# A new order for the first 300 steps of a hand-ordered kernel, and another place in PSUM for the state update's products

## The chip, the cores and the metric

The kernel runs on one core of one Trainium2 chip. The time is the device time of one execution in microseconds (us); the median of several runs is compared. A profile, taken in one execution, tells for each engine when every instruction ran: TensorE (PE; its weight loads are PEld), VectorE (DVE), ScalarE (ACT), GpSimd (POOL), and SyncE (SP), whose queue issues all the transfers here.

## The reference

Two blocks follow each other. The first is a gated linear attention with a state per batch and head (4 batches, 8 heads, 768 positions, 48 wide); the second is an MLP over the 3072 tokens (384 to 2048 to 384) with a hard-swish.

```python
for t in range(S):
    state = alpha[:, :, t, :, None] * state + einsum('bhd,bhe->bhde', k[:, :, t], v[:, :, t])
    y[:, :, t] = einsum('bhd,bhde->bhe', q[:, :, t], state)
x = y.transpose(0, 2, 1, 3).reshape(B * S, H * D)
h = x @ w_in
g = h * clip(h + 3.0, 0.0, 6.0) / 6.0
out = g @ w_out
```

The weights arrive as 64-bit floats, and the kernel turns them into 32-bit floats itself, by integer operations on their bits.

## The kernel before, in words

**Chunks.** The recurrence goes in 24 chunks of 128 positions (6 for each batch), numbered j, with all 8 heads in a chunk. A scan over alpha (line 309, `r.j`) gives the products of decays from the end of the chunk, a second scan (line 320, `p.j`) those from its start. k is multiplied by the one (`k.j`), q by the other (`q.j`, both line 332). The scores of the two halves of a chunk (`sc.j`, line 346) are masked (`m.j`, line 356), and `ya.j` and `yb.j` (line 455) multiply values and state by scores and queries. The state goes on by `u.j` (line 429: products of k by token and v, for both halves), `sm.j.b` (lines 437 and 439: the sum with the old state), `st.j` (line 409, on GpSimd: the decay) and `sv.j.b` (line 419: the state put beside the values).

**The first six chunks** differ from the others. Their alpha, k and q are loaded in natural order (`la`, `lk`, `lq`, line 251, 1024 packets of 192 bytes) and turned by TensorE (`ta`, `tk`, `tq`, line 282); `ca.j` copies the turned alpha out of PSUM on ScalarE (line 300), `kb.j` turns k back (line 374) and `ck.j` copies it (line 378). `lv.j` loads the values, `qa.j.b` places queries (line 366).

**Weights.** 16 slices (`w.i`) are loaded into five raw buffers used in turn, so that a later slice waits until an earlier one is done. `d2.i` (magnitude, line 196), `d1.i` (low word, line 186) and, for slices 0, 1, 2 and 4, `dx.i` (sign, line 191) run on ScalarE; `d3.i` on VectorE (lines 203 and 205 for these four, lines 207, 208 and 210 for the others); `d4.i` on GpSimd (line 217) adds the low bits and finishes the slice.

**MLP.** For the first chunk pairs the hidden layer is computed by `fa`, `fb`, `f.g.i` (lines 489 and 478), with `fr` on ScalarE (line 494) and `fg` on VectorE (line 498); `b.c.part` (line 516) is the second product. Later pairs use sums of blocks with fewer products (`M`, `P` and others, lines 600 and 703). `z.m.n` issues n products of an identity matrix whose result nobody reads (line 532).

**What sets the order.** The whole kernel is one list of 1788 words, each of which is a step. Steps are emitted in the order of the list, and each engine, and SP's queue of transfers, takes its own instructions strictly in that order; waits between engines follow from the data. So the list is the schedule, and nothing else decides on it.

**PSUM.** Four banks (`banks`, 512 columns each) serve the recurrence: turned chunks (all columns), scores (columns 0 to 255), the state update's products (columns 0 to 191) and y. A number at the end of a word names the bank (`sc.1.0.2` puts the scores of chunk 1 into banks 0 and 2). Four others serve the MLP. Whoever writes columns waits for the reader of what was there. In `update`, two halves of a chunk go to two banks.

Of the kernel before, what the change touches and what calls it, by code (L numbers as in the profile page):

```python
# [17 lines left out]
def kernel(  # L18
# [33 lines left out]
    B, H, S, D = q.shape  # L52
# [4 lines left out]
    NP = H // 2  # L57
# [3 lines left out]
    G = 2  # L61
    GT = G * C
    HB = C // 2
# [157 lines left out]
    R_t, P_t, Q_t, K_t, kb_t, A_t, xT_t, ps_t = ({} for _ in range(8))  # L221
# [200 lines left out]
    def update(j, *at):  # L422
        for b, i in enumerate(at):
            ps_t["u", j, b] = banks[i][:, 0 : NP * D].rearrange("r (p n) -> r p n", p=NP)
        for p in range(NP):
            for a in range(2):
                for b in range(len(at)):
                    half = slice(HB * b, HB * b + HB)
                    nc.tensor.matmul(ps_t["u", j, b][64 * a : 64 * a + D, p],  # L429
                                     kb_t[j][half, p, 64 * a : 64 * a + D],  # L430
                                     v_t[j][half, b, 2 * p + a, 0:D],
                                     start=True, stop=True)
# [316 lines left out]
    def run(words):  # L749
        for word in words.split():  # L750
            name, *at = word.split(".")
            steps[name](*(int(x) for x in at))

    with tc.manual_schedule():
        run("""z.0.5 z.0.3 z.0.1 z.0.8 qa.0.0 w.0 d2.0 d3.0 la.0 ta.0.0 ca.0 r.0 lk.0 tk.0.1 k.0
               z.0.2 p.0 la.1 ta.1.2 lq.0 tq.0.3 ca.1 r.1 lk.1 lv.0.0 sv.0.0 d1.0 kb.0.0 ck.0 z.0.2
               u.0.2.1 sm.0.0 sv.0.1 q.0 qa.0.1 tk.1.0 k.1 p.1 z.0.2 sc.0.2.3 m.0 la.2 ta.2.0 ca.2
               dx.0 w.2 d2.2 kb.1.0 ck.1 lq.1 r.2 sm.0.1 st.1 tq.1.2 q.1 d3.2 z.0.3 d1.2 dx.2
               lv.1.1 u.1.3.1 sv.1.0 sm.1.0 p.2 sm.1.1 sc.1.0.2 m.1 ya.0.3 yb.0 cy.0 lq.2 w.1 d1.1
               tq.2.1 q.2 d4.2 lk.2 tk.2.3 k.2 fa.2.0 d4.0 st.2 sc.2.0.2 d2.1 d3.1 m.2 dx.1 d4.1  # L760
               qa.1.1 lk.3 la.3 ta.3.1 ca.3 la.4 fa.0.1 sv.1.1 w.3 r.3 ta.4.3 ca.4 r.4 tk.3.1 k.3
               kb.2.0 qa.1.0 d2.3 ya.1.2 yb.1 cy.1 fa.1.2 lq.3 ck.2 d1.3 p.3 d3.3 lv.2.2 u.2.3.2
               sm.2.0 d4.3 fb.2 tq.3.1 q.3 fb.1 qa.2.0 sm.2.1 sv.2.0 st.3 fr.0.2.0 fg.0.2 lk.4
               tk.4.0 sv.2.1 w.5 d2.5 k.4 d3.5 d1.5 qa.3.0 d4.5 qa.2.1 sc.3.1.3 m.3 w.6 d2.6 d1.6
               d3.6 d4.6 lv.3.0 lq.4 w.7 kb.3.2 fb.0 f.0.3.3 kb.4.0 ya.2.1 ck.3 u.3.3.2 sm.3.0
               fr.0.3.1 fg.0.3 fr.0.1.0 fg.0.1 qa.3.1 sv.3.0 sm.3.1 p.4 d2.7 sv.3.1 d1.7 d3.7 d4.7
               f.0.5.0 fr.0.5.1 fr.0.0.0 fg.0.5 fg.0.0 tq.4.3 ck.4 la.5 ta.5.2 f.0.6.3 ca.5 w.4
               d2.4 ya.3.0 yb.3 cy.3 fr.0.6.1 yb.2 cy.2 w.9 d2.9 q.4 qa.4.1 d1.4 d1.9 dx.4 la.6 w.8
               d3.4 r.5 lk.5 w.10 d3.9 p.5 ca.6 fg.0.6 d4.9 w.12 lq.5 lv.4.1 d2.8 d3.8 f.0.7.2 d1.8
               st.4 d4.8 d4.4 w.11 fr.0.7.0 fg.0.7 f.1.7.0 fr.1.7.1 fg.1.7 sc.4.0.2 m.4 f.1.1.1  # L770
               fr.1.1.0 fg.1.1 f.1.3.3 fr.1.3.1 d2.10 d1.10 tk.5.3 f.1.0.2 d2.12 d3.10 d4.10 w.13
               fg.1.3 fr.1.0.0 fg.1.0 k.5 d3.12 lq.6 f.1.6.0 f.1.2.1 u.4.1.0 sm.4.0 d1.12 d4.12
               sv.4.0 qa.4.0 ya.4.2 fr.1.6.1 fg.1.6 w.15 tq.5.3 fa.4.3 sv.4.1 d2.11 kb.5.1 d2.13
               fr.1.2.0 f.1.4.2 fr.1.4.1 d1.11 sm.4.1 q.5 r.6 d3.11 d3.13 fg.1.4 d4.11 lv.5.0 lk.6
               tq.6 p.6 d2.15 d3.15 fg.1.2 d1.13 d4.13 sc.5.0.3 yb.4 f.1.5.0 fr.1.5.1 fg.1.5 tk.6
               m.5 b.1.0.2 fb.4 b.1.1 d1.15 d4.15 st.5 y.5 w.14 la.7 lk.7 cy.4 d2.14 qa.5.1 ck.5
# [3 lines left out]
               lv.6.2 ck.6 u.6.3.0 s.1.3.2 x.2 P.1.2 b.0.3 K.1.1 y.7 s.1.4 s.1.5 y.11 y.3 r.7  # L780
               xc.2.1 x.3 y.4 y.8 xc.2.3 k.7 xc.2.0 xc.2.4 y.9 y.12 y.16 y.13 y.15 P.1.3.3 K.1.2
               P.1.4 bo.1 P.1.5 xc.2.5 G.1.1.1 P.1.6 y.14 y.17 y.19 xc.2.6 sm.6.0 G.1.2.2 y.20
               M.2.0.2 lv.12.1 la.8 O.1.1 O.1.0 ca.8 y.18 y.21 y.23 so.1 G.1.3.3 n.2.0.8 bo.0 lq.7
               lv.7.0 O.1.2 m.6 xc.2.2 xc.2.10 xc.2.7 tq.7 r.8 p.7 xc.2.8 sv.6.1 M.2.15.3 M.2.1
               kb.7.3 n.2.1.9 M.2.16 M.2.2 n.2.2.10 M.2.7.0 n.2.7.11 sm.6.1 xc.2.9 q.7 p.8 M.2.3
               M.2.4 n.2.4.12 M.2.8 o.2.0.0 M.2.5 n.2.5.13 qa.7.0 sv.6.0 st.7 lk.8 O.1.3 lq.8 lk.9
               la.9 la.10 tk.8 tq.8 lq.10 lq.9 ya.6.1 yb.6 M.2.9 z.1.3 M.2.18.1 o.2.1.0 e.2.1.1
               M.2.10 cy.6 ck.7 sc.7.0.2 u.7.1.3 n.2.10.14 M.2.11 qa.7.1 ca.9 la.11 y.22 M.2.6.2
               h.2.1 q.8 m.7 e.2.0.0 h.2.0 n.2.11.15 qa.6.0 n.2.18.10 qa.8.1 M.2.12 M.2.19
               n.2.12.12 M.2.13 sm.7.0 sv.7.1 r.9 k.8 o.2.3.0 sv.7.0 ya.7.0 y.24 o.2.5.0 n.2.13.12  # L790
               o.2.2.0 yb.7 cy.7 sc.8.1.2 xc.3.1 o.2.2.1 e.2.2.1 xc.3.3 o.2.3.1 M.2.14 xc.3.4
               xc.3.0 xc.3.5 o.2.4.0 xc.3.7 xc.3.6 o.2.6.0 P.2.0.1 M.3.0.2 M.2.17 h.2.2 o.2.6.1
               e.2.3.0 h.2.3 o.2.7.0 n.3.0.12 M.3.1 n.3.1.9 e.2.5.1 M.3.7.0 n.3.7.13 xc.3.8 o.2.7.1
               K.2.0.3 xc.3.2 kt.8 e.2.6.0 h.2.6 tk.9 M.3.2 n.3.2.10 e.2.4.0 P.2.1 h.2.4 h.2.5
               s.2.0.14 e.2.7.0 G.2.0.1 h.2.7 M.3.3 M.3.4 n.3.4.8 k.9 s.2.1.11 M.3.8 o.3.0.0 ca.10
               kt.9 P.2.3.3 s.2.2.15 s.2.3.14 lv.8.2 kw.8 kr.8 lk.10 sm.7.1 xc.3.9 M.3.5 n.3.5.11
               K.2.2 e.3.0.1 xc.3.10 M.3.9 o.3.1.0 P.2.2 K.2.1 u.8.0.3 M.3.18.2 s.2.5 M.3.10
               n.3.10.14 n.3.18.15 e.3.1.0 s.2.4 P.2.4 tq.9 h.3.0 st.8 sv.8.0 M.3.11 n.3.11.8 tk.10
               p.9 sm.8.0 q.9 r.10 k.10 qa.9.0 qa.9.1 m.8 sm.8.1 h.3.1 M.3.19 o.3.5.0 kt.10 P.2.5
               G.2.2.0 st.9 M.3.12 sc.9.0.1 qa.8.0 n.3.12.10 o.3.3.0 kw.9 lv.9.0 kr.9 sv.8.1  # L800
               u.9.2.3 sm.9.0 sv.9.1 sv.9.0 G.2.1.2 sm.9.1 st.10 M.3.15.2 M.3.16 M.3.6.3 M.3.13 m.9
               o.3.4.0 o.3.6.0 tq.10 n.3.13.10 o.3.2.0 e.3.4.1 ya.8.2 yb.8 ya.9.3 yb.9 cy.9 M.3.14
               M.3.17 cy.8 xc.4.1 P.2.6 e.3.5.0 G.2.3.3 o.3.2.1 xc.4.3 h.3.4 xc.4.4 o.3.6.1 xc.4.5
               xc.4.0 xc.4.6 e.3.2.1 M.4.0.0 n.4.0.10 P.3.0.1 xc.4.7 o.3.7.0 p.10 h.3.5 o.3.3.1
               xc.4.8 M.4.7.3 M.4.1 xc.4.2 h.3.2 o.3.7.1 K.3.0.2 lk.11 O.2.2 tk.11 e.3.6.0 e.3.3.1
               h.3.3 P.3.1 e.3.7.1 n.4.1.13 M.4.2 ca.11 q.10 h.3.6 r.11 k.11 h.3.7 n.4.7.15 lv.10.2
               lv.11.0 kw.10 sc.10.0.1 kr.10 G.3.0.0 u.10.3.2 sm.10.0 qa.10.1 n.4.2.14 M.4.3 M.4.4
               M.4.8 s.3.0.9 xc.4.9 s.3.2.12 s.3.1.11 P.3.3.2 n.4.4.8 M.4.5 o.4.0.0 e.4.0.0 sv.10.1
               sm.10.1 xc.4.10 kt.11 O.2.0 O.2.3 lq.11 m.10 s.3.3.9 s.3.5 M.4.9 o.4.1.0 P.3.2
               sv.10.0 st.11 n.4.5.11 K.3.2 la.13 M.4.18.0 p.11 tq.11 lk.12 tk.12 K.3.1 M.4.10  # L810
               n.4.10.9 q.11 qa.10.0 n.4.18.12 e.4.1.1 la.12 s.3.4 ca.12 h.4.0 r.12 P.3.5 G.3.2.1
               h.4.1 M.4.11 P.3.4 n.4.11.8 M.4.12 n.4.12.14 qa.11.0 M.4.19 p.12 G.3.1.3 lq.12 kw.11
               O.2.1 tq.12 kr.11 u.11.3 sc.11.0.2 sv.11.0 O.3.1 lk.13 P.3.6 qa.11.1 M.4.6.2 G.3.3.2
               k.12 o.4.3.0 m.11 sm.11.0 sv.11.1 kt.12 M.4.13 n.4.13.14 q.12 o.4.3.1 e.4.3.0
               o.4.2.0 o.4.6.0 h.4.3 o.4.2.1 ya.10.1 ya.11.0 yb.10 yb.11 cy.11 cy.10 xc.5.1 ca.13
               xc.5.3 M.4.15.1 M.4.16 M.4.14 P.4.0.2 o.4.4.0 M.4.17 xc.5.4 o.4.5.0 xc.5.0 xc.5.5
               M.5.0.0 o.4.6.1 K.4.0.3 e.4.2.1 h.4.2 P.4.1 qa.12.1 e.4.4.0 xc.5.6 o.4.7.0 h.4.4
               o.4.7.1 tk.13 n.5.0.14 M.5.1 e.4.7.1 h.4.7 e.4.5.0 xc.5.2 h.4.5 xc.5.7 G.4.0.3
               e.4.6.1 h.4.6 s.4.1.12 s.4.0.11 xc.5.8 r.13 xc.5.9 xc.5.10 k.13 kw.12 kr.12 la.14
               sc.12.2.3 u.12.0.1 sm.12.0 n.5.1.13 M.5.2 n.5.2.15 M.5.7.1 n.5.7.8 P.4.3.3 s.4.2.9  # L820
# [118 lines left out]
```

## Time and profile before

| | us |
|---|---|
| median of 3 runs | 537.83 (537.21 to 538.51) |
| the profiled execution's own time | 537.71 |
| its span, first to last instruction | 535.6 |
| PE busy | 523.6 (98%) |
| DVE busy | 475.1 (89%) |
| ACT busy | 259.7 (48%) |
| POOL busy | 50.4 (9%) |

Between the span and the execution's own time lie 2.1 us in which no instruction of the program runs. Busy shares are means over the span; the stage that the change touches is the first 90 us of it, and there the engines must be read window by window and instruction by instruction. Successive instructions of one engine overlap a little, so the distance from start to start is what counts in a queue. The granted clock of PE is 1.00 throughout in the profile's rows.

### The profile page before, as it was taken

How to read it: one execution, taken by the hardware profiler on the slowest of the kernel's cores; microseconds unless marked ns; L12 is line 12 of the kernel's file. 1: busy time of each engine (PE TensorE's matmuls, PEld its weight loads, DVE VectorE, ACT ScalarE, POOL GpSimd, SP SyncE). 2: the span in 40 equal slices, each digit the busy share in tenths (PEclk: the TensorE clock that was granted, in tenths of full speed). 3: DMA queues.
4: the chain of work that ended last, by engine and by line, in shares of the span. 5: the costliest groups of instructions: out<-in, count | busy, mean ns of one | idle time of the engine just before them, and what ended most of it. 6: DMA issues, size and time to landing. Idle time of an engine off the chain costs nothing.

```text
span 535.6 us, 15166 instructions
## 1 busy us (share of the span) xinstructions
PE 523.6 (98%) x6306; PEld 497.0 (93%) x6306; DVE 475.1 (89%) x839; ACT 259.7 (48%) x513; POOL 50.4 (9%) x71
## 2 busy tenths in 40 slices
PE   7799999999999999999999999999999999999997
PEld 7698886789999999999999999999999999999996
DVE  6999989999999899989999899999999898595381
ACT  3889864302753644543644444642634545553240
POOL 5333435000000000000010000000000000000000
PEclk9999999999999999999999999999999999999999
DMA  9998877006515155254354355055354042100001
GB/s 175 214 250 263 205 218 164 9 1 162 151 28 121 29 120 134 51 139 90 92 118 104 89 122 141 20 126 124 85 137 103 17 97 48 43 3 1 15 16 37
DMA packets 124100, 54.40 MB, mean 102 GB/s; under 512 B 83328, under 2 KB 116864, under 8 KB 124032
## 3 DMA queue, kind: packets, MB, share of 16 engines
q1 hardware_dynamic: 124032, 53.44, 42.4%
q8 instruction: 49, 0.80, 0.7%
q14 instruction: 19, 0.16, 0.1%
HBM read 44.50 MB, written 8.91 MB: 100 GB/s over the span
## 4 chain that ended last, share of the span: by engine, by line
PE 64%; DVE 20%; SPq 5%; DMA 3%; issue 3%; ACT 2%; POOL 2%; DVEq 0%; ACTq 0%; POOLq 0%
PE m_ps L703 28%; PE m_ps L600 24%; PE m_ps L478 4%; SPq L262 3%; PE t_ps L455 3%; DVE R L309 2%; DVE g_sb L498 2%; DVE A L356 2%; DMA v<-in_v_dram 1%; PE t_ps L346 1%; PE m_ps L516 1%; PE t_ps L429 1%; DVE g_sb L537 1%; DVE q L332 1%; DVE t L286 1%
## 5 line engine op out<-in xcount | busy, mean ns | idle before, releaser
L703 PE MATMUL m_ps<-w,g_sb 128*128 128x192 f32 x704 | 122.1, 327 | 0.7 <-ACT m_ps L709 0.6
L606 ACT COPY g_sb<-m_ps 128x512 f32<-128x512 f32 x110 | 63.5, 584 | 113.8 <-PE m_ps L600 97.4
L703 PEld LDWEIGHTS m_ps<-w,g_sb 128*128 128x128 f32 x704 | 113.7, 190 | 1.8 <-ACT m_ps L709 0.9
L703 PE MATMUL m_ps<-rings,g_sb 128*128 128x192 f32 x528 | 91.6, 327 | 0.6 <-ACT u L682 0.6
L703 PEld LDWEIGHTS m_ps<-rings,g_sb 128*128 128x128 f32 x528 | 85.3, 190 | 1.0 <-ACT u L682 0.9
L600 PE MATMUL m_ps<-xc,w 128*128 128x128 f32 x640 | 82.8, 277 | 0.5 <-DVE w L541 0.5
L600 PEld LDWEIGHTS m_ps<-xc,w 128*128 128x128 f32 x640 | 77.5, 192 | 1.7 <-issue 0.6
L494 ACT ACTIVATE r<-g_sb,half 128x512 f32<-128x512 f32 x80 | 56.7, 722 | 29.5 <-DVE g_sb L541 11.7
L498 DVE SCALAR_TENSOR_TENSOR g_sb<-r,g_sb 128x512 f32<-128x512 f32 x80 | 53.6, 683 | 7.2 <-ACT r L494 6.8
L600 PE MATMUL m_ps<-xT,raw 128*128 128x128 f32 x400 | 52.6, 278 | 1.0 <-ACT g_sb L606 0.9
L600 PEld LDWEIGHTS m_ps<-xT,raw 128*128 128x128 f32 x400 | 48.6, 192 | 2.0 <-ACT g_sb L606 1.4
L409 POOL TENSOR_TENSOR st<-sm,R 128x192 f32<-128x192 f32 x20 | 12.9, 644 | 354.4 <-DVE sm L439 305.6
L647 DVE TENSOR_TENSOR g_sb<-g_sb 128x512 f32<-128x512 f32 (+1 forms) x55 | 42.0, 792 | 1.4 <-PE m_ps L703 1.1
L600 PE MATMUL m_ps<-xT,w 128*128 128x128 f32 x320 | 42.0, 276 | 0.0
L600 PEld LDWEIGHTS m_ps<-xT,w 128*128 128x128 f32 x320 | 39.3, 192 | 0.1
L366 ACT COPY A<-q 48x256 f32<-48x256 f32 x88 | 35.6, 404 | 4.9 <-DVE q L332 3.7
L356 DVE TENSOR_TENSOR A<-t_ps,mask 64x256 f32<-64x256 f32 x96 | 36.0, 413 | 0.4
L478 PE MATMUL m_ps<-xT,w 128*128 128x256 f32 x144 | 32.8, 382 | 0.1
L600 PE MATMUL m_ps<-xc,raw 128*128 128x128 f32 x240 | 31.8, 276 | 0.0
L309 DVE TENSOR_TENSOR_SCAN R<-t,ones 128x516 f32<-128x516 f32 x24 | 29.6, 1235 | 1.1 <-ACT t L300 1.0
L478 PEld LDWEIGHTS m_ps<-xT,w 128*128 128x128 f32 x144 | 26.7, 190 | 3.8 <-POOL w L217 0.2
L600 PEld LDWEIGHTS m_ps<-xc,raw 128*128 128x128 f32 x240 | 29.6, 192 | 0.1
(105 smaller groups left out, 724.8 us busy)
## 6 DMA issues: line engine op xcount, KB each, us to landing
raw<-in_moe_w_out_dram SPq DMA_DIRECT2D x8, 768.0 KB, 5.2
raw<-in_moe_w_in_dram SPq DMA_DIRECT2D x6, 768.0 KB, 6.7
v<-in_v_dram SPq DMA_DIRECT2D x48, 96.0 KB, 3.0
out_dram<-oh SPq DMA_DIRECT2D x44, 96.0 KB, 1.7
far<-kq SPq DMA_DIRECT2D x64, 64.0 KB, 2.2
kb<-far SPq DMA_DIRECT2D x64, 64.0 KB, 2.0
aq<-in_alpha_dram SPq DMA_DIRECT2D x36, 96.0 KB, 2.4
qq<-in_q_dram SPq DMA_DIRECT2D x36, 96.0 KB, 2.4
```

The source lines that it names most:

```text
L262: nc.sync.dma_start(out=to[BLK * o : BLK * (o + 1), :, 0 : V * D - skip], in_=t[o // 2, :, :, skip : V * D])
L309: nc.vector.tensor_tensor_scan(out=reverse(R, n - 1, n), data0=reverse(ax, n, n), data1=reverse(ones, n, n), initial=0.0, op0=ALU.mult, op ...
L356: nc.vector.tensor_tensor(out=to[:, a], in0=sc[a][half], in1=mask[half, half].unsqueeze(1).to_broadcast([HB, NP, HB]), op=ALU.mult)
L366: nc.scalar.copy(out=to[:, a], in_=Q_t[j][64 * a : 64 * a + D, :, half])
L455: nc.tensor.matmul(y_of(j, (i + 1) // 2, p)[:, HB * b : HB * b + HB], vb[:, p, e : e + 32], A_t[j][:, b, 2 * p + a], start=(b == 0 and i = ...
L478: nc.tensor.matmul(h[:, f], w1[:, kk, o : o + C], xT_t[g][:, kk], start=(kk == 0), stop=(kk == KT - 1))
L494: nc.scalar.activation(out=to, in_=h, func=AF.Relu, bias=half, scale=1.0 / 6.0)
L498: nc.vector.scalar_tensor_tensor(out=to, in0=r, scalar=1.0, in1=h, op0=ALU.min, op1=ALU.mult)
L600: nc.tensor.matmul(acc[g][i][:, f * C : (f + 1) * C], spots[w][:, f * C : (f + 1) * C], x_of(g, x), start=(first and f == 0), stop=last, s ...
L606: nc.scalar.copy(out=slots[z], in_=acc[g][i])
L647: nc.vector.tensor_tensor(out=out, in0=in0, in1=in1, op=ALU.subtract)
L703: nc.tensor.matmul(to[g], a, rhs[:, f], start=(first and f == 0), stop=(last and f == HF - 1), skip_group_check=True)
```

## The change

The first 300 of the 1788 words are put into another order; the multiset of steps is the same but for the banks named in 30 of them (`ta`, `tk`, `tq`, `kb`, `sc`, `u`, `ya`), and the remaining 1488 words are unchanged. In `update` the products are put into columns 256 to 447 of their banks instead of 0 to 191.

```diff
     def update(j, *at):
         for b, i in enumerate(at):
-            ps_t["u", j, b] = banks[i][:, 0 : NP * D].rearrange("r (p n) -> r p n", p=NP)
+            ps_t["u", j, b] = banks[i][:, NP * HB : NP * (HB + D)].rearrange(
+                "r (p n) -> r p n", p=NP)
...
-        run("""z.0.5 z.0.3 z.0.1 z.0.8 qa.0.0 w.0 d2.0 d3.0 la.0 ta.0.0 ca.0 r.0 lk.0 tk.0.1 k.0
-               z.0.2 p.0 la.1 ta.1.2 lq.0 tq.0.3 ca.1 r.1 lk.1 lv.0.0 sv.0.0 d1.0 kb.0.0 ck.0 z.0.2
-               u.0.2.1 sm.0.0 sv.0.1 q.0 qa.0.1 tk.1.0 k.1 p.1 z.0.2 sc.0.2.3 m.0 la.2 ta.2.0 ca.2
-               dx.0 w.2 d2.2 kb.1.0 ck.1 lq.1 r.2 sm.0.1 st.1 tq.1.2 q.1 d3.2 z.0.3 d1.2 dx.2
-               lv.1.1 u.1.3.1 sv.1.0 sm.1.0 p.2 sm.1.1 sc.1.0.2 m.1 ya.0.3 yb.0 cy.0 lq.2 w.1 d1.1
-               tq.2.1 q.2 d4.2 lk.2 tk.2.3 k.2 fa.2.0 d4.0 st.2 sc.2.0.2 d2.1 d3.1 m.2 dx.1 d4.1
-               qa.1.1 lk.3 la.3 ta.3.1 ca.3 la.4 fa.0.1 sv.1.1 w.3 r.3 ta.4.3 ca.4 r.4 tk.3.1 k.3
...
-               st.4 d4.8 d4.4 w.11 fr.0.7.0 fg.0.7 f.1.7.0 fr.1.7.1 fg.1.7 sc.4.0.2 m.4 f.1.1.1
-               fr.1.1.0 fg.1.1 f.1.3.3 fr.1.3.1 d2.10 d1.10 tk.5.3 f.1.0.2 d2.12 d3.10 d4.10 w.13
-               fg.1.3 fr.1.0.0 fg.1.0 k.5 d3.12 lq.6 f.1.6.0 f.1.2.1 u.4.1.0 sm.4.0 d1.12 d4.12
-               sv.4.0 qa.4.0 ya.4.2 fr.1.6.1 fg.1.6 w.15 tq.5.3 fa.4.3 sv.4.1 d2.11 kb.5.1 d2.13
-               fr.1.2.0 f.1.4.2 fr.1.4.1 d1.11 sm.4.1 q.5 r.6 d3.11 d3.13 fg.1.4 d4.11 lv.5.0 lk.6
-               tq.6 p.6 d2.15 d3.15 fg.1.2 d1.13 d4.13 sc.5.0.3 yb.4 f.1.5.0 fr.1.5.1 fg.1.5 tk.6
-               m.5 b.1.0.2 fb.4 b.1.1 d1.15 d4.15 st.5 y.5 w.14 la.7 lk.7 cy.4 d2.14 qa.5.1 ck.5
+        run("""lk.0 la.0 la.1 z.0.8 z.0.3 w.0 ta.0.2 z.0.5 ca.0 r.0 d2.0 tk.0.1 k.0 lq.0 z.0.2 la.2
+               ta.1.2 kb.0.1 z.0.2 w.2 lk.1 w.1 p.0 z.0.3 d3.0 d1.0 lv.0.0 ca.1 ta.2.3 r.1 ck.0
+               tq.0.2 ca.2 lq.1 q.0 lk.2 tk.1.0 dx.0 sc.0.1.2 d2.2 sv.0.0 r.2 lv.1.1 qa.0.1 p.1 d1.2
+               z.0.2 la.3 k.1 d2.1 d4.0 m.0 d3.2 ya.0.0 u.0.3.1 dx.2 sm.0.0 kb.1.3 d3.1 sm.0.1
+               sv.0.1 tq.1.2 yb.0 q.1 d1.1 cy.0 lq.2 ck.1 p.2 tk.2.1 st.1 sc.1.2.0 w.3 u.1.3.0
+               sm.1.0 dx.1 fa.0.1 ta.3.3 k.2 sv.1.0 d4.2 fa.2.0 qa.1.0 ca.3 m.1 lv.2.2 lk.3 kb.2.2
+               sv.1.1 sm.1.1 w.5 r.3 qa.1.1 d4.1 lq.3 st.2 tq.2.1 q.2 ya.1.0 yb.1 d2.3 p.3 cy.1
...
+               fr.1.3.1 d1.8 k.5 fr.1.1.0 d2.12 fg.1.1 f.1.6.0 f.1.2.1 lk.7 d4.4 ck.4 lv.4.1
+               fr.1.0.0 d3.12 d4.8 lv.5.0 u.4.2.0 sc.4.3.0 sc.5.2.1 d1.12 fg.1.3 ca.6 w.11 d4.12
+               st.4 fa.4.3 fr.1.6.1 fg.1.6 fg.1.0 d2.11 m.4 f.1.4.2 fb.4 f.1.5.0 w.15 sm.4.0 r.6
+               d1.11 d4.10 fr.1.4.1 sv.4.1 d2.15 d3.11 m.5 sv.4.0 fg.1.4 b.1.0.2 fr.1.2.0 d3.15 w.13
+               d4.11 w.14 d2.13 lq.6 lk.6 p.6 b.1.1 fr.1.5.1 d3.13 d1.13 sm.4.1 d1.15 ya.4.3 yb.4
+               d4.15 fg.1.5 tq.6 kb.5.0 fg.1.2 d4.13 tk.6 st.5 y.5 z.0.1 cy.4 d2.14 qa.5.1 ck.5
                b.0.0.1 fr.0.4.0 d3.14 k.6 q.6 ca.7 fg.0.4 d1.14 d4.14 x.0 y.1 y.10 b.0.1 y.0 y.2
...
```

Both lists hold 26 of the identity products of `z`. In the list of before the first words of the DMA queue are w.0, la.0, lk.0, la.1, lq.0, lk.1, lv.0; in the new one they are lk.0, la.0, la.1, w.0, lq.0, la.2, w.2, lk.1, w.1, lv.0.

## The prediction

> **What bounds the kernel now.** First view: the page's busy table, then the table of windows over the first 160 us, because only the first 300 of 1788 steps are reordered (they end near 90 us).
>
> ```profile
> PE 523.6 (98%) x6306; PEld 497.0 (93%) x6306; DVE 475.1 (89%) x839; ACT 259.7 (48%) x513; POOL 50.4 (9%) x71
> 10.00:20.00 10.00, 6.87 (x103) 5.46 (x104) 9.75 (x18) 7.30 (x12) 0.04 (x1) 1.00 1.30 234
> 50.00:60.00 10.00, 9.93 (x164) 8.24 (x163) 9.80 (x15) 9.74 (x15) 4.63 (x5) 1.00 0.79 226
> 100.00:110.00 10.00, 10.00 (x156) 6.44 (x155) 10.00 (x14) 1.67 (x4) 0.00 (x0) 1.00 0.01 2
> ```
>
> In the rows the columns are PE, PEld, DVE, ACT, POOL busy of 10 us, clock, DMA share and GB/s. DVE is at 97% or more from 10 us on; PE has room only in the first two rows. Second view, the waits: what PE and DVE wait for up to 160 us, and PE's two late waits in the timeline.
>
> ```profile
> DVE w L203 <- ACT w L196: 2.4, 1, 2.4
> DVE s L439 <- PE t_ps L429: 1.2, 1, 1.2
> DVE R L309 <- ACT t L300: 1.0, 1, 1.0
> 127.84 0.91 PE L600 MATMUL m_ps<-xc,w 128*128 128x128 f32 x6 [0.47 <-DVE w L541]
> 156.44 1.73 PE L703 MATMUL m_ps<-w,g_sb 128*128 128x192 f32 x9 [0.16 <-ACT m_ps L709]
> ```
>
> DVE, once started, is idle for 0.96 us (before 9.26) and 1.16 us (before 72.38), then not at all until 157, and PE's only waits between 52 and 157 are for DVE's results or for ACT behind them. So DVE's place in its queue at step 300 is carried to 157, and PE, which is nearly without a gap behind that, carries it to the end. PE alone being early gives nothing beyond the 0.47 that it waits at 127.
>
> Third view, POOL beside DVE.
>
> ```profile
> 81.22 1.18 DVE L320 TENSOR_TENSOR_SCAN P<-t 128x516 f32<-128x516 f32 x1
> 82.32 1.75 DVE L207 TENSOR_SCALAR w<-w 128x768 f32<-128x768 f32 x1
> 81.65 2.01 POOL L217 TENSOR_TENSOR w<-raw 128x768 int32<-128x768 int32 x1 [0.19 <-POOL kq L257]
> 28.03 1.86 POOL L217 TENSOR_TENSOR w<-w,raw 128x768 int32<-128x768 int32 x1 [0.75 <-ACT raw L191]
> 29.36 1.62 DVE L309 TENSOR_TENSOR_SCAN R<-t,ones 128x516 f32<-128x516 f32 x1
> 89.98 0.55 DVE L207 TENSOR_SCALAR w<-w 128x768 f32<-128x768 f32 x1
> ```
>
> L217 (d4) came up during a scan, ran when the scan ended, and L207, otherwise 0.55 to 0.61, took 1.75: DVE stood still until POOL was done. The scan at 29.36 lost 0.40 in the same way (1.62 against 1.22). The scores' mask (L356), L332 and L498, which read PSUM, keep their duration beside L217.
>
> **The budget of DVE.** From d3.0 (6.57) to d3.14, step 306 (89.98), are 83.41 us. In them: idle 0.96 + 1.16; lost to POOL 0.40 (r.3), 0.39 (d3.1: first op 1.09 for 0.70), 1.14 (d3.15), and 0.28 (d3.0's first op, 0.98 for 0.70, beside POOL's memsets). Sum 4.33, so the work is 79.1. The new order has the same DVE steps. Its start: the first loads are now k, alpha, alpha, then w.0, so d3.0 can no longer run ahead of r.0 in the time in which DVE has nothing else. PE starts with z.0.8 and z.0.3, 22 passes, at 1.47. The first pass takes 0.375 and the next ones 0.213 each (they drop to 0.112 at 6.96), so ta.0 starts at 1.84 + 21 x 0.213 = 6.3; three of its four passes are slow, the last starts at 6.96. ca.0 came 0.31 after that pass before, and takes 0.59: r.0 at about 7.9 (9.26 before). The alpha load is second of three small ones, 1.2 us apart in the landings of before, and is there near 5. DVE would end at 7.9 + 79.1 = 87.0 if it never waited; before it was 89.98. **The new order may wait 3.0 us before it loses.**
>
> A sentence for the rule that speaks on this start: the Trainium skill, "TensorE: Matmul & The Clock Gate", Part 1, puts the change to full rate around 4 us into sustained matmuls, give or take 0.5; by it (5.5 instead of 6.96) r.0 would start some 0.6 earlier, an estimate from that page. Here the passes change 5.5 us after the first, and the row is taken.
>
> **The waits of the new order**, walked from start-to-start rows (r 1.36 to 1.5, p 1.14, k and q 0.60, halves d3 1.36, m 1.50, sm 0.27):
> - a) d4.0. DVE: r.0 7.9, k.0 9.3, p.0 9.9, d3.0 11.0, r.1 12.4, q.0 13.8, r.2 14.4, p.1 15.8. ACT: ta.2 stands behind kb.0, which needs k.0 (9.9): 10.05 + 0.47 + two fillers of 0.45 and 0.67 = 11.6; ca.2 12.25, dx.0 (1.94) to 14.8. So L217 comes up in r.2's scan, as at 81.65, and p.1 waits. Between 0 (ready after 15.8, then it runs beside k.1 and m.0, which read PSUM) and 1.86 (all of L217). By the d3.15 row, 1.14 of a 1.47 L217: 1.5 of 1.86.
> - b) sm.1.0 after p.2: u.1 now waits for ck.1, behind sv.0.1, d1.1 and cy.0 on ACT: 0.71 + 0.93 + 0.48 + 0.58 after sm.0.0, and 0.63 from u's start to sm. 0 to 0.7; 0.6.
> - c) r.3 against d4.1, which stands behind d4.2 on POOL: 0 to 1.2; 0.4 as before.
> - d) d4.15 stands ahead of d4.13 now and waits for d1.15; it comes up near 84, inside d3.13's three ops (83.4 to 85.6). 0 to 1.4; by the d3.15 row 1.2.
> - e) small ones (m.2, d3.9 for w.9, whose load waits for d4.6 on SP, q.5, m.4): 0.2 with a), 1.0 without, since DVE then arrives earlier.
> The 1.16 wait for u.4 goes: u.4 is ahead of fa.4 and f.1.4 as before, but sm.4.0 is now behind m.4. What is late next there is sc.4, which stands behind u.4 on PE and which m.4 needs; it is in e).
> Sum 3.9: DVE reaches d3.14 at 90.9, **0.9 later**.
>
> The other queues. PE: 26 fillers before and after, at no cost. It is idle 4.7 us up to 31 us before; afterwards fa.0 starts at 24.6 without a), 26.1 with it, and counting the products behind (f 2.7, fa 1.34) PE is 0.7 earlier or 0.3 later at tk.4. SP: the loads land in the order of issue; the set up to la.5 that landed by 44.15 is the same set up to lq.4, so DMA gains nothing as a whole. lv.0 goes from seventh place of the loads to tenth, landing near 18.4 (13.2 before); that is covered, since ya.0 waits for m.0 (19 or later); uncovered it costs up to 5 us. w.14 now stands before lq.6 and lk.6 on SP and waits for d4.11 (near 79); they land by 87, tq.6 and tk.6 need them from 87 on: 0 to 0.5, taken as 0.
>
> Column 256: no instruction more or less. A u may be written beside scores that wait for their mask. In steps 301 to 1788 nothing waited for that bank, as PE's waits there name DVE's w and g_sb, ACT's g_sb, m_ps and u (a kept sum) alone: 0, within 0.1 either way.
>
> **Rivals.**
> 1. POOL's additions miss the scans: dx.0 ends after 15.8 and d4.15 outside d3.13. For it: a shift of ACT against DVE by 1 us is enough for the first, and most L217 before ran beside steps that read PSUM (28.03 under m.2 until the scan came). Against: both are needed. DVE's waits fall to 0.6 to 2.2, but PE's 0.7 plus the 0.47 of slack limit the gain to 1.2: 536.6. Chance 0.20.
> 2. One of a) and d) is absent: without a) the waits are 3.4 (b 0.7, c 0.5, d 1.2, e 1.0), without d) 2.7, so 0.4 later or 0.3 earlier: 537.5 to 538.2. Chance 0.16.
> 3. Slower: p.2 loses to d4.2. st.1 starts 0.51 after sm.0.1 and runs 0.52; d4.2 stands directly behind it, at 1.02. p.2 arrives at 0.27 + 0.60 = 0.87, during st.1. If POOL goes on without a gap, p.2 waits all of d4.2, 1.7; it decides whether p.2 starts before 1.02. Against: at 26.6 a DVE op that waited went ahead of the next L409. 0.9 + 1.7: 540.4. Chance 0.20.
> 4. PE runs at half rate again. Between the filler behind sc.0 (16.0) and ya.0 (19.1, or 20.6 with a) PE has nothing for 3.1 to 4.6 us; before, its longest idle stretch was 0.96, and the rate stayed at 0.112. If slow passes (0.213) come back for the 5.5 us of the start, PE loses up to 2.7, of which three transposes (0.4 each) lie on DVE's path at least: 1.2 to 2.7, taken as 2.0. 0.9 + 2.0: 540.7. Chance 0.14. The Trainium skill, the same page, "HAM oscillation", warns of idle gaps over 3.4 us; no run here shows one yet.
> That the reorder has no effect at all can't be: the first load already differs.
>
> **How the numbers follow.** The forecast, a) to e) as valued, has 0.30. The profiled execution took 537.71 (span 535.6 and 2.1 around it), 0.12 under the median 537.83; 0.9 on the median is 538.7. About 0.2% (1.08 us) is what can be told from no change. The forecast's own range is 537.9 to 539.4 (b, c, e at their ends), so a third of its chance is beyond 538.9: 0.10 slower, 0.20 same. Same: 0.20 + 0.16 = 0.36. Slower: 0.10 + 0.20 + 0.14 = 0.44. Faster: 0.20. The range takes in half of rivals 1 and 4: 536.5 to 540.7.
>
> **What would show it.** The first scan of DVE near 7.9; the second p's start behind a L217 near 17 rather than at 15.8; a d3 with an op of 1.7 to 2.0 near 84; d3.14 near 91; PE's wait at 127 larger. Wrong, if no scan stands beside L217 (rival 1), if a scan after st.1 starts after 26 (rival 3), or if passes near 21 us are 0.213 apart (rival 4).

## The result and the profile after

The changed kernel took 541.27 us, the median of 6 runs (540.04 to 542.88), against 537.75 (537.21 to 538.51) for the kernel before on the same chip: a ratio of 1.0070 with a 95% interval of 1.0058 to 1.0083. The forecast was 538.7, its range ended at 540.7. The profiled execution of after took 540.35, with a span of 538.3.

First the table of windows of after. The columns are PE, PEld, DVE, ACT and POOL busy, the granted clock, the DMA share and GB/s.

```profile
10.00:20.00 10.00, 6.43 (x117) 5.15 (x117) 9.73 (x15) 9.13 (x12) 1.97 (x1) 0.75 1.21 247
20.00:30.00 10.00, 8.98 (x157) 7.94 (x150) 9.01 (x16) 7.11 (x13) 4.74 (x4) 0.73 1.11 231
40.00:50.00 10.00, 9.56 (x105) 7.97 (x105) 9.78 (x18) 8.34 (x16) 2.93 (x2) 1.00 0.49 112
```

The granted clock was 1.00 in these rows before. Now it is 0.75 and 0.73: the records have it at half from 15.1 to 25.3 us. The third row shows the DMA engines half idle between 40 and 50 us, which matters further down. The waits that DVE makes up to 95 us, "what for" behind the arrow, with total, count and longest:

```profile
DVE R L309 <- ACT t L300: 2.9, 2, 2.7
DVE g_sb L499 <- ACT r L495: 0.7, 1, 0.7
DVE w L207 <- ACT w L196: 0.6, 1, 0.6
DVE q L332 <- PE t_ps L282: 0.5, 1, 0.5
DVE s L440 <- PE t_ps L430: 0.2, 1, 0.2
```

The first line is mostly the start (2.70 before the first scan at 6.88). Waits tell only half: what POOL takes shows as long instructions. The timeline of after, DVE and POOL:

```profile
14.30 1.97 POOL L217 TENSOR_TENSOR w<-w,raw 128x768 int32<-128x768 int32 x1 [6.73 <-ACT raw L191]
14.77 2.60 DVE L320 TENSOR_TENSOR_SCAN P<-t 128x516 f32<-128x516 f32 x1
23.31 0.69 DVE L332 TENSOR_TENSOR q<-t_ps,P 128x512 f32<-128x512 f32 x1 [0.48 <-PE t_ps L282]
23.38 1.84 POOL L217 TENSOR_TENSOR w<-w,raw 128x768 int32<-128x768 int32 x1
24.03 2.28 DVE L320 TENSOR_TENSOR_SCAN P<-t 128x516 f32<-128x516 f32 x1
26.48 0.36 DVE L440 TENSOR_TENSOR s<-t_ps,st 128x192 f32<-128x192 f32 x1 [0.17 <-PE t_ps L430]
85.46 1.46 POOL L217 TENSOR_TENSOR w<-raw 128x768 int32<-128x768 int32 x1 [2.51 <-ACT raw L186]
85.51 1.83 DVE L207 TENSOR_SCALAR w<-w 128x768 f32<-128x768 f32 x1
92.84 0.55 DVE L207 TENSOR_SCALAR w<-w 128x768 f32<-128x768 f32 x1
```

Three times a DVE instruction stands still for more than 1 us until an L217 ends: p.1 at 14.77 and p.2 at 24.03 (2.52 and 2.45 to the next start, 1.14 where nothing holds them) and d3.13's first at 85.51 (1.87, 0.59 otherwise). Behind p.2, sm.1.0 (26.48) still waits 0.17 for u.1, whose products do not need p.2: with p.2 short and PE no faster, sm.1.0 would hardly have come earlier. The last row is d3.14, step 306: 92.84, which is 2.86 later than before. Third, PE in the timeline of after:

```profile
14.48 0.66 PE L282 MATMUL t_ps<-ident,rings 128*128 128x128 f32 x4 [2.38 <-DMA rings<-in_k_dram]
16.13 1.22 PE L533 MATMUL m_ps<-ident 128*128 128x128 f32 x4
21.30 1.11 PE L374 MATMUL t_ps<-ident,k 128*128 128x128 f32 x4 [1.01 <-DVE s L438]
22.21 1.06 PE L282 MATMUL t_ps<-ident,rings 128*128 128x128 f32 x4
91.45 3.81 PE L517 MATMUL m_ps<-w,g_sb 128*128 128x384 f32 x11 [1.05 <-DVE g_sb L499]
```

PE waits 2.38 for the load of k of chunk 1, and from 15.1 on four passes take 1.06 to 1.22 in place of 0.60 to 0.66. At 91.45 it waits 1.05 for DVE's fg.1.2; the same product started at 88.20 before. Of these 3.24 us PE makes up some 0.5: the product P.2.0.1 starts at 151.66 (148.91 before) and the last, P.11.6, at 532.67 (529.92), both 2.75 later. The wait of 0.47 at 127 that PE had before is gone.

So the delay that DVE has near d3.14 is carried to the end, and it arises before that step. It is not carried as predicted: the prediction looked for a longer wait of PE at 127, but PE is late from 91.45 on and has no wait in the profile between there and 159. Over all the profiles that follow, the profiled execution's time is 537.3 plus the delay of d3.14 against 89.98, within 0.25 us.

### The profile page after: what moved, and what is told of

Read it like the earlier page. It is cut to its first block, busy times and chain, and to the rows that moved or that the text cites. A ratio compares the mean times of both kernels' runs of the same rounds, so it can differ in the third digit from the quotient of the medians.

```text
span 538.3 us, 15147 instructions
## 1 busy us (share of the span) xinstructions
PE 524.8 (97%) x6306; PEld 497.9 (92%) x6306; DVE 477.0 (89%) x839; ACT 259.5 (48%) x513; POOL 50.3 (9%) x71
## 3 DMA queue, kind: packets, MB, share of 16 engines
q1 hardware_dynamic: 124032, 53.44, 42.2%
## 4 chain that ended last, share of the span: by engine, by line
PE 69%; DVE 14%; DMA 6%; SPq 4%; ACT 3%; issue 3%; POOL 0%; DVEq 0%; ACTq 0%; POOLq 0%
PE m_ps L704 32%; PE m_ps L601 25%; PE t_ps L456 3%; PE m_ps L517 3%; SPq L262 3%; DVE g_sb L499 2%; PE m_ps L490 2%; DMA g_sb<-in_moe_w_in_dram 2%; PE t_ps L346 1%; PE t_ps L430 1%; ACT r L495 1%; DMA raw<-in_moe_w_in_dram 1%; DVE g_sb L538 1%; DVE A L356 1%; DVE R L309 1%
## 5 line engine op out<-in xcount | busy, mean ns | idle before, releaser
L495 ACT ACTIVATE r<-g_sb,half 128x512 f32<-128x512 f32 x80 | 56.7, 722 | 30.1 <-DVE g_sb L542 11.7
L320 DVE TENSOR_TENSOR_SCAN P<-t 128x516 f32<-128x516 f32 x24 | 31.8, 1326 | 0.2
```

The costliest lines, as they stand in the source:

```text
L320: nc.vector.tensor_tensor_scan(out=P_t[j], data0=aX[j % 2][:, 0:n], data1=ini[j % 2], initial=0.0, op0=ALU.mult, op1=ALU.add)
L495: nc.scalar.activation(out=to, in_=h, func=AF.Relu, bias=half, scale=1.0 / 6.0)
```

## The experiments

Every kernel below the first row was timed in five rounds beside the kernel before on the same chip, whose medians were 537.27, 537.34 and 537.49. The third column is against the one that goes with the run. The last three columns are from the one profiled execution: the first scan of DVE (r.0), d3.14, and the mean granted clock.

| kernel | median us | against before | ratio, 95% interval | r.0 at | d3.14 at | clock |
|---|---|---|---|---|---|---|
| after | 541.27 | +3.52 | 1.0070 [1.0058, 1.0083] | 6.88 | 92.84 | 0.990 |
| after_again | 540.77 | +3.43 | 1.0062 [1.0050, 1.0074] | 7.16 | 93.51 | 0.991 |
| col256_only | 537.36 | +0.09 | 1.0001 [0.9992, 1.0009] | 9.38 | 89.89 | 1.000 |
| fill_pe | 539.74 | +2.47 | 1.0045 [1.0029, 1.0061] | 8.03 | 92.69 | 1.000 |
| late_dx0 | 540.18 | +2.91 | 1.0053 [1.0041, 1.0065] | 7.81 | 92.52 | 0.994 |
| d415_last | 541.16 | +3.89 | 1.0067 [1.0053, 1.0082] | 7.35 | 91.88 | 0.990 |
| no_d40_d42 | 538.65 | +1.31 | 1.0014 [1.0001, 1.0027] | 7.33 | 91.63 | 0.994 |
| loads | 539.89 | +2.55 | 1.0044 [1.0029, 1.0059] | 6.85 | 91.49 | 0.990 |
| pause_pool | 540.66 | +3.17 | 1.0053 [1.0038, 1.0067] | 7.77 | 94.75 | 0.991 |
| all_four | 538.36 | +1.02 | 1.0017 [1.0008, 1.0025] | 7.25 | 90.74 | 1.000 |
| five | 536.98 | -0.51 | 0.9987 [0.9978, 0.9996] | 7.75 | 89.15 | 1.000 |
| five_less_fill | 537.69 | +0.20 | 1.0001 [0.9992, 1.0010] | 7.83 | 90.55 | 0.997 |
| before_no_fill | 538.12 | +0.63 | 1.0013 [1.0004, 1.0022] | 8.62 | 90.73 | 0.994 |

In after, after_again and the nine kernels from fill_pe to five_less_fill nothing ahead of r.0 differs, and yet r.0 comes anywhere from 6.85 to 8.03. It goes with the moment at which PE gets its full rate, which the clock records put at 4.79 in loads (r.0 at 6.85), at 4.86 in after (6.88) and at 7.68 in fill_pe (8.03). So d3.14 of two rows can't be compared without r.0, and the single medians differ from that of after by little more than their intervals; gains below about 1 us are estimates.

### The two parts of the change: col256_only

The order of before with the products in columns 256 to 447.

```diff
-            ps_t["u", j, b] = banks[i][:, 0 : NP * D].rearrange("r (p n) -> r p n", p=NP)
+            ps_t["u", j, b] = banks[i][:, NP * HB : NP * (HB + D)].rearrange(
+                "r (p n) -> r p n", p=NP)
```

> The order of before with the column change alone. If the column place costs or gains anything by itself, the time moves by a good part of the 3.5 us between the two kernels (540 or more). If the order alone does it, 537.75 within 0.5. I expect the second.

537.36 against 537.27, within an interval of some 0.5 us. In the old order the column costs nothing that can be told, so the loss is put down to the order; the column was not tested in the new order alone.

### PE's clock: fill_pe

Two groups of identity products are put where PE waits: ten behind tq.0, and ten in place of two behind sc.0.

```diff
-               tq.0.2 ca.2
+               tq.0.2 z.0.10 ca.2
...
-               z.0.2 la.3
+               z.0.10 la.3
```

> The changed kernel with 10 identity products more behind tq.0, where PE waited 2.4 us for k of chunk 1, and 10 instead of 2 behind sc.0, where it waited for the mask. If the half clock of PE between 15.1 and 25.3 us is a main cost, the granted clock reads 1.00 throughout, passes near 21 us are 0.11 apart instead of 0.21, q.1 no longer waits (0.48) and the time falls by 1 to 2 us, to 539 to 540; the spread of the runs shrinks too. If GpSimd's additions beside the scans are all of it, the clock reads 1.00 and the time stays within 0.4 of the changed kernel's 541.3.

The windows of fill_pe, columns as above, and its p.2 in the timeline:

```profile
10.00:20.00 10.00, 9.06 (x132) 8.55 (x131) 9.87 (x15) 9.07 (x11) 2.25 (x1) 1.00 1.22 245
20.00:30.00 10.00, 7.93 (x178) 7.14 (x175) 9.79 (x18) 7.49 (x14) 4.39 (x3) 1.00 1.05 214
```

```profile
24.33 1.87 POOL L217 TENSOR_TENSOR w<-w,raw 128x768 int32<-128x768 int32 x1
24.40 2.88 DVE L320 TENSOR_TENSOR_SCAN P<-t 128x516 f32<-128x516 f32 x1
```

The half rate is gone, so the cause of it was PE's idle time. The clocks of the other executions agree: 0.997 to 1.000 in all six of fill_pe, 0.990 or 0.991 in all six of after. The gain is about 1.0 of 3.5 in the medians; the spread did not shrink as expected (538.04 to 541.52). The profile's d3.14 is only 0.15 earlier, but its r.0 came 1.15 later, so from r.0 on 1.30 are gained. Part is lost again: with PE at full rate p.2 arrives right behind the start of d4.2 and waits for all of it (2.81 to the next start instead of 2.45), and d3.12 waits 0.49 for slice 12.

### The locks one by one: late_dx0, d415_last, no_d40_d42, pause_pool

late_dx0 moves dx.0 behind d2.2 on ACT, so that d4.0 is ready later.

```diff
-               tk.1.0 dx.0 sc.0.1.2 d2.2 sv.0.0
+               tk.1.0 sc.0.1.2 d2.2 dx.0 sv.0.0
```

> The changed kernel with dx.0 behind d2.2 on ACT, so that d4.0 comes up near 16.2, while p.1 runs, and not while r.2 does. If GpSimd's addition held p.1 back, p.1 takes 1.14 instead of 2.52 from start to start, the mask of chunk 0 starts near 16.5 instead of 17.9, and the time falls by about 1.4 us or more (PE's idle stretch ahead of ya.0 is shorter as well); 539.9. If the loss is the clock alone, p.1 is short but the time stays within 0.4 of 541.3.

p.1 is free (1.12 to the next start, at 15.47 with L217 behind it at 15.72), and m.0 comes 0.70 earlier (17.18), although r.0 came 0.93 later. But d3.15 comes only 0.27 earlier (82.04) and the median gains about 0.5 where 1.4 were expected, inside the intervals. The timeline of late_dx0 shows p.1, and where the rest went:

```profile
15.47 1.21 DVE L320 TENSOR_TENSOR_SCAN P<-t 128x516 f32<-128x516 f32 x1
57.94 0.69 DVE L499 SCALAR_TENSOR_TENSOR g_sb<-r,m_ps 128x512 f32<-128x512 f32 x1 [0.53 <-ACT r L495]
69.78 0.56 DVE L207 TENSOR_SCALAR w<-w 128x768 f32<-128x768 f32 x1 [0.43 <-ACT w L196]
```

At fg.0.6 (57.94) DVE is still 0.71 ahead of after. Then d3.12 (69.78; 69.98 in after) waits 0.43 for slice 12, whose load SP issued at 63.66 (62.28 in after): DVE came earlier, the slice did not. That need not come from the edit: in after_again, the unchanged kernel, slice 12 was issued at 64.91 and d3.12 waits 0.71.

d415_last puts d4.15 behind d4.13.

```diff
-               d4.15 fg.1.5 tq.6 kb.5.0 fg.1.2 d4.13 tk.6
+               fg.1.5 tq.6 kb.5.0 fg.1.2 d4.13 d4.15 tk.6
```

> The changed kernel with d4.15 behind d4.13 on GpSimd, so that it does not stand beside d3.13. If d4.15 held VectorE up there, d3.13's first operation takes 0.6 instead of 1.83 and everything behind it is 1.2 us earlier: 540.1. If PE is the bound at that place, the operation is short and the time the same, 541.3.

In the profile d3.13 keeps its 0.6, d3.14 is 0.96 earlier and the execution took 539.03. That was the fastest of its six, and the median, 541.16 where 540.1 was expected, is no better than that of after. The profile shows the lock removed; that this alone gains time is not shown.

no_d40_d42 leaves out d4.0 and d4.2, and with them the low bits of weight slices 0 and 2: a bound for what the locks at p.1 and p.2 cost together.

```diff
-               d2.1 d4.0 m.0
+               d2.1 m.0
...
-               sv.1.0 d4.2 fa.2.0
+               sv.1.0 fa.2.0
```

> The changed kernel without GpSimd's additions d4.0 and d4.2: the low bits of weight slices 0 and 2 are left out, nothing else. If these two additions beside p.1 and p.2 cost what VectorE stood still for them (1.4 and 1.1), p.1 and p.2 take 1.14 each and the time falls by 2.5, to 538.8. If a later wait is a floor that takes early gains back (in the three variants so far VectorE comes to d3.15 at 82.0 to 82.3 whatever it gained before), VectorE is 2 us or more earlier at m.2 (35.8 in the changed kernel), but again at 82 at d3.15, and the time falls by less than 1.

m.1 comes at 25.75 (27.36 in after), the median falls by 2.1, more than any other single edit gives, although the clock is still at half from 16.0 to 22.9. Behind it waits appear that after does not have, or has at less than 0.2: 0.79 for sm.1.0, 0.51 for r.3, 0.49 for q.3, 0.52 for fg.0.5. The single executions range from 535.95 to 539.58, the widest spread of all the kernels.

pause_pool puts seven small memsets of a spare tile on POOL between st.1 and d4.2, so that p.2 can start first.

```diff
+    spare_pool = consts.tile([C, 64], FP, tag="spare_pool", name="spare_pool")
+    def pause(n):
+        for _ in range(n):
+            nc.gpsimd.memset(spare_pool, 0.0)
...
-               st.1 sc.1.2.0
+               st.1 zp.7 sc.1.2.0
```

> The changed kernel with seven small memsets of a tile of their own on GpSimd between st.1 and d4.2 (0.8 us), so that p.2 asks first and d4.2 runs behind it, beside sm.1.0, k.2 and m.1, which read PSUM. If p.2 loses to d4.2 only because d4.2 starts 0.6 us ahead of it, p.2 takes 1.14 instead of 2.28 from start to start, m.1 starts 0.8 to 1.1 earlier, and the time falls by up to 1.1; by less, near 0.3, if the loads for d3.9 and d3.12 hold VectorE back again. If the memsets themselves hold the scan, p.2 takes 2 or more.

The timeline of pause_pool, DVE and PE:

```profile
24.71 1.23 DVE L320 TENSOR_TENSOR_SCAN P<-t 128x516 f32<-128x516 f32 x1
27.69 0.36 DVE L440 TENSOR_TENSOR s<-t_ps,st 128x192 f32<-128x192 f32 x1 [1.75 <-POOL w L217]
26.84 0.69 PE L430 MATMUL t_ps<-v,kb 64*48 64x48 f32 x32
```

The scan takes 1.23 again, and the next step, sm.1.0, waits 1.75. The view names POOL because L217 ended last; but sm.1.0 needs u.1, which PE ended at 27.53, and it does not need the slice: in five, below, it starts 0.08 after an L217 did, and in after, five and five_less_fill as here it starts 0.15 to 0.16 after u.1's last product ended. So the half clock holds DVE at sm.1.0 with p.2 free, as the 0.17 in after already said. The two causes lie over each other there, and neither fill_pe nor pause_pool can win much alone. How long the wait is depends on the execution: here the half rate ran from 16.95 to 27.19, later than in after, and m.1 came later, not earlier as expected. (The profiled execution, 541.98 with d3.14 at 94.75, was the longest of its five.)

### The gate at slice 9: loads

w.9 behind lq.5, and la.6 ahead of d4.9.

```diff
-               sm.3.0 w.9 m.3
+               sm.3.0 m.3
...
-               lq.5 yb.3
+               lq.5 w.9 yb.3
...
-               la.7 d4.9 la.6
+               la.7 la.6 d4.9
```

> The changed kernel with two loads moved in SP's queue: w.9, which waits for d4.6, behind w.4, lk.5 and lq.5, and la.6 ahead of d4.9 in the list, so that w.12 does not stand behind it. If the loads are the floor, the waits of d3.9 (0.56), fg.0.6 (0.69) and d3.12 shrink by 1 us or more in all and VectorE comes to d3.15 before 81.5; the time falls by 0.5 to 1.2. If they are not, d3.15 stays at 82 or later and the time within 0.4 of 541.2.

In after, w.9 waits on SP for d4.6, with every later load behind it: it is issued at 47.19 and landed at 53.44, and the third row of after's windows shows the DMA engines idle meanwhile. In the timeline of loads the same two steps (before the first, 0.56 of waiting in after, before the second 0.69) have no wait:

```profile
53.72 0.56 DVE L207 TENSOR_SCALAR w<-w 128x768 f32<-128x768 f32 x1
57.41 0.69 DVE L499 SCALAR_TENSOR_TENSOR g_sb<-r,m_ps 128x512 f32<-128x512 f32 x1
```

d3.15 comes at 81.15 in place of 82.31, with r.0 and the half rate at the same place as in after (6.85, and 15.03 to 25.27). The median gains about 0.9. This is the cleanest pair of profiles here.

### All together: all_four, five, and one filler less

all_four joins fill_pe, late_dx0, d415_last and loads; five adds the seven memsets; five_less_fill is five with z.0.2 instead of z.0.10 behind sc.0.

> The changed kernel with the four edits together: more identity products, dx.0 behind d2.2, d4.15 behind d4.13, and the two loads moved. If early delays, floor and d4.15 act one after the other, it gains more than the sum of the single ones (1.3, 0.9, 0.2 and that of the loads): d3.15 before 81, d3.14 near 89.5 to 90.5, 537.0 to 538.3, about the kernel before. If something else keeps VectorE back, d3.15 stays at 82 and the time above 539.

all_four is still 1.02 over before, just outside what was expected. p.2 comes 0.08 behind d4.2 now and loses all of it, and sm.2.1 waits 1.74 for u.2, in the midst of which PE stands 1.84 without a wait that the profile shows.

> The kernel with four edits and this pause as a fifth. In the one with four, p.2 came 0.08 us behind d4.2 and stood still for 1.7 us. If the pause flips that, p.2 takes 1.14, and d3.14 comes near 89.0 unless the 1.7 us wait of sm.2.1 on PE stays: 90 with it. 536.5 to 537.5: level with the kernel before or 0.1% below it. If something else bounds, d3.14 stays at 90.7 and the time at 1.0017 of before.

The timeline of five, POOL and DVE:

```profile
22.61 1.40 POOL L737 MEMSET spare_pool<- 128x64 f32 x7
23.97 3.66 POOL L217 TENSOR_TENSOR w<-w,raw 128x768 int32<-128x768 int32 x2
22.71 1.23 DVE L320 TENSOR_TENSOR_SCAN P<-t 128x516 f32<-128x516 f32 x1
24.05 0.36 DVE L440 TENSOR_TENSOR s<-t_ps,st 128x192 f32<-128x192 f32 x1
```

p.2 runs its 1.23 beside the memsets, and d3.14 comes at 89.15, 3.69 before that of after and 0.83 before that of before. The median, 536.98, is 0.13% under the kernel before (interval 0.04% to 0.22%), which is below the 0.2% named as what can be told from no change: level with it, perhaps a little faster. PE's 1.84 within u.2 is absent here, although PE has the same instructions as in all_four, so not all of the difference between these two is the memsets'. Against after the five edits are worth 3.9 to 4.0 (3.43 or 3.52 over before, and 0.51 under it).

> The same five edits with only the identity products behind tq.0 and 2, not 10, behind sc.0. If the 1.84 us in which PE issued nothing inside u.2 came from the place at which those 16 more passes put it in PE's instruction stream, it is gone or elsewhere, and sm.2.1 does not wait. If PE's clock needs both groups, a half-rate stretch is back and the time is 1 us above the kernel with both.

537.69 against 536.98 for five on the same chip: one group of eight identity products more is worth about 0.7 (the two intervals just meet). The window row of five_less_fill shows why:

```profile
20.00:30.00 10.00, 9.36 (x180) 8.48 (x184) 8.00 (x15) 7.74 (x15) 6.02 (x11) 0.83 1.03 238
```

q.1 waits 0.48 and sm.1.0 waits 0.89 for PE again. The granted clock is 1.000 in all eleven executions of five and 0.994 to 0.999 in those of five_less_fill.

### Fillers in the old order: before_no_fill

The kernel before without its four groups behind r.0 (nine products).

> The kernel before without the four groups of identity products behind r.0 (9 products, 2.2 us of PE up to 19 us). If sparse work on PE is what brings the half rate, PE reads 0.5 in a stretch between 12 and 26 us, and the time rises by 0.5 to 2 us. If the rate falls only after PE stands still for most of a 3.4 us stretch, which before's longest idle stretch (0.96, about 1.7 without the products) does not come near, it stays at 1.00 and the time within 0.4 of before.

It loses 0.63. The windows of before_no_fill, and PE's longest wait in its timeline:

```profile
10.00:20.00 10.00, 5.13 (x89) 3.78 (x90) 9.16 (x17) 7.32 (x12) 0.04 (x1) 0.97 1.30 234
20.00:30.00 10.00, 9.87 (x198) 9.32 (x199) 9.39 (x19) 9.16 (x13) 6.34 (x5) 0.69 1.01 215
```

```profile
19.94 1.03 PE L429 MATMUL t_ps<-v,kb 64*48 64x48 f32 x29 [1.62 <-ACT kb L378]
```

The clock is at half from 19.35 to 26.17, and the mean is 0.987 to 0.994 in all eleven executions (0.997 to 1.000 in those of before). So the old order stands on its fillers too. The half rate is not a property of the new order but of any start in which PE is left idle enough.

### The spread: after_again

The kernel after, unchanged.

> The changed kernel once more, for a second profile: its runs lie between 540.0 and 542.9, and the profiled one was at the low end with 2.75 us of delay at the end of PE's chain. If the rest of the spread comes from where the windows of PE's clock fall, the half-rate stretch begins at another time than 15.1 and the delay at d3.14 differs from 2.86 with it; if it comes from somewhere behind 100 us, d3.14 is at 92.8 again and the span differs.

540.77; its ratio of 1.0062 lies in the interval of the first time. Its d3.14 is at 93.51, with the half rate from 15.67 to 25.91 and with 0.94 before fg.0.6 and 0.71 before d3.12: at least part of the differences from run to run arises before step 306.

## Why the prediction was wrong, by its own steps

**What held.** DVE's budget up to d3.14 was the right account; the delay there was carried to the end, though through PE from 91.45 on and not through a wait at 127; column 256 costs nothing in the old order; POOL's L217 does come up in r.2's scan and inside d3.13. The Trainium skill, "SBUF — State Buffer", "SBUF: two separate sides", says that a VectorE instruction in a two-port mode, or one with two inputs from SBUF where the GpSimd instruction reads SBUF, shares one pair of ports with GpSimd as an exclusive lock, and that the second to start fully blocks. The trace agrees: instructions 2.60, 2.28 and 1.83 long for 1.23, 1.23 and 0.55, while the scan beside the memsets, which read nothing, kept its 1.23.

**The sum.** From its first scan DVE took 85.96 to d3.14 (6.88 to 92.84); with 79.1 of work that is 6.86 of waiting, against 3.9 forecast.

| term | forecast us | measured us |
|---|---|---|
| start of r.0 | 7.9 | 6.88 |
| a) d4.0 at p.1 | 1.5 | 1.38 |
| b) sm.1.0 for u.1 | 0.6 | 0.17 |
| c) r.3 | 0.4 | 0.16 |
| d) d4.15 at d3.13 | 1.2 | 1.28 |
| e) small ones | 0.2 | 2.25 (r.4 beside L217 0.35, d3.9 0.56, fg.0.6 0.69; 0.65 is left, in pieces below 0.2) |
| rival 3, d4.2 at p.2 | 0 | 1.14 |
| rival 4, q.1 for PE at half rate | 0 | 0.48 |

Of the 2.96 us by which the waiting was put too low, e) makes up 2.05 and the two rivals 1.62; a), b) and c) were put 0.79 too high. The 1.14 of rival 3 is what p.2 lost, not what its removal would gain, since b) would take its place.

**First failed step: the rivals.** Rivals 3 and 4 were set against the forecast and against each other, with 0.20 and 0.14. Both came, together with a) and d). They are not alternatives: nothing in a), d) or rival 4 keeps rival 3 away. Rival 3 itself hung on 0.15: p.2 was put at 0.87 after sm.0.1's start and d4.2 at 1.02. In fill_pe, at full rate, they were 0.97 (0.26 and 0.71, where 0.60 was taken for q.1) and 0.90, so p.2 came 0.07 late; in after, where rival 4 adds 0.48 ahead of q.1, it came 0.65 late. So p.2 lost already without rival 4, and with it there was no margin left at all. The margin of 0.15 was too thin to bet four in five on. The sign set for rival 3, a scan that starts after 26, could not come so: a scan that is held is recorded as started (24.03) and as long (2.28).

**Second: the price of rival 4, and its place.** It was looked for behind the filler at 16.0; the rate fell at 15.1, after PE's 2.38 of waiting for k of chunk 1. That wait was not in the walk at all. Behind the filler, where 3.1 to 4.6 were expected, PE waited 1.03. The 2.0 was too much: fill_pe, which removes the half rate, gained about 1.0 in the medians, and in its profile p.2 and slice 12 took part of the gain. The warning of the Trainium skill, "TensorE: Matmul & The Clock Gate", "HAM oscillation", of idle gaps over 3.4 us, which the prediction names, was no bound here: no single gap was that long.

**Third, and by size the largest: e).** w.9 was named with its wait for d4.6 and then valued with others at 0.2. It is the head of SP's queue, and it cost DVE 0.56 and, through ACT, 0.69; without these waits, in loads, d3.15 came 1.16 earlier. Slice 12 is a second gate, from run to run a wider or a narrower one: late_dx0 lost 0.43 there of the 0.71 that DVE was ahead, fill_pe waited 0.49 and after_again 0.71, while in after and in loads d3.12 does not wait. The single edits add up to less than all of them together (1.0, 0.5, 0.9 and 0.3 by the medians, nothing for d415_last, against 3.9). That fits these gates and the overlap at p.2, but each gain is uncertain by about 1 us, so the shortfall itself is not shown.

**The start** was off in the other direction. The full rate came at 4.86, 3.4 after the first pass, not 5.5 after it, and r.0 at 6.88. The Trainium skill, "TensorE: Matmul & The Clock Gate", Part 1, speaks of a free-running window of about 3.4 us whose phase varies from run to run. Here the full rate came between 4.8 and 7.7 in the profiles, 3.3 to 6.2 after the first pass, which is a wider spread than the 0.5 either way that the prediction took from that page. For this execution the page's value was nearer, and one row was not enough to set it aside. Over the eleven profiles with this start r.0 lay between 6.85 and 8.03, so 7.9 was a possible value, and the 1.0 that the start gave back in this execution was luck.

**The account of the miss.** 1.94 too late at d3.14 (3.0 more waiting, 1.0 less start) makes 1.74 in the profiled execution (538.61 expected of it, 540.35 found). The other 0.8 is that the median of after lies 0.92 above its profiled execution, where 0.12 had been allowed: the new order varies more from run to run (540.04 to 542.88) than the old one (537.21 to 538.51). A half rate of another length is not the reason, since the granted clock is 0.990 or 0.991 in all six. The place of r.0 can be part of it, as the profiled execution had one of the earliest; no run shows how much.

**What stays open.** Why the medians of after, loads and d415_last lie 0.9, 1.1 and 2.1 above their profiled executions: only one execution of each is seen. Why PE stood 1.84 within u.2 in all_four and not in five. Whether p.2 meets d4.2 in the runs that were not profiled.

## What to carry to other kernels

Ask of every unfavourable case whether it can come together with the others, and give the sum of those that can a chance of its own; where a case is decided by a margin of 0.15 us between two in-order queues, its chance is near a half, not one in five. Before an early gain is added up, look for the next gate behind it (here a load that waits at the head of SP's queue), for it can take part of the gain away. Before two profiles are compared, see whether both began alike (here r.0 varied by 1.2). And two stalls that lie over each other at one step show nothing when one is removed: remove both before calling either harmless.

## What the runs showed of the hardware that was not expected

The TensorE clock falls to half without one long gap: in after 2.38 us of idle time in the 3.4 before it fell (11.7 to 15.1) was enough. In before_no_fill it fell at 19.35, in the midst of PE's longest gap after 10 us (1.62); of the 3.4 before, PE had been idle 1.9, in three pieces of 0.68, 0.20 and the 1.0 of that gap so far. It then stays at half for 3.4 us (five_less_fill: 0.83 over 10 us), 6.8 (late_dx0: 17.0 to 23.8) or 10.2 (after: 15.1 to 25.3), that is, in multiples of some 3.4 us. Eight more identity products in the right place, which nobody reads, are worth about 0.7 us here (five against five_less_fill).
